# Gate, up and the gradient of h in one loop per 512 columns, half of the rows at a time, with relu(gate) and masked up kept in SBUF

## The chip, the cores and the metric

One core of a Trainium2 chip runs the whole program. The metric is the device time of one execution in microseconds (us). TensorE (PE) multiplies and transposes into PSUM, ScalarE (ACT) and VectorE (DVE) read PSUM and do the elementwise work, GpSimd (POOL) does little, and SyncE's queue (SP) issues nearly all DMAs, strictly in program order. For this kernel a difference under about 0.5% (11 us) can't be told from no change.

## The reference, cut to what matters

Forward and backward of a block with two branches on xn = layernorm(x), with S = 2048 rows, D = 1024 and F = 3584, all in bf16. The change is in branch B and its surroundings.

```python
gate = xn @ W_gate;  up = xn @ W_up              # [S, F]
h = relu(gate) * up
out = x + A(xn, k, v, ...) + h @ W_down
# backward, g = grad_out:
gh = g @ W_down.T                                # gradient of h, [S, F]
g_up = gh * relu(gate);  g_gate = gh * (gate > 0) * up
gW_down = h.T @ g;  gW_gate = xn.T @ g_gate;  gW_up = xn.T @ g_up
gx = ... + g_gate @ W_gate.T + g_up @ W_up.T     # through the layer norm
```

A is a shift convolution of k, a product with v, a long convolution over S (done as matrix Fourier transforms) and a product with xn, with its own gradients. It runs in 8 groups of 128 channels.

## The kernel before

Rows go in 16 tiles of 128 (`st`), D in 8 tiles of 128 (`kt`), F in 7 blocks of 512 columns (`fb`). A product of one row tile with one block is 8 matmuls of 512 columns into one PSUM tile (`gemm8`, L581). Four PSUM tiles (`b_ps`) go round for all of branch B.

Branch B goes through these phases, in this order: `layer_norm` (L520), `gate_up` (L589), `grad_hidden` (L611), `grad_down` (L667, gradient of W_down), `grad_in` (L685, gradients of W_gate and W_up), `out_phase` (L718, output 0) and `grad_x` (L753, gradient of x).

- `layer_norm` goes over chunks of 1, 1, 2, 4, 4 and 4 row tiles: two passes on ACT per tile (L537, L544), short steps on DVE, the scaling (L560), a store of xn to DRAM from POOL's queue (L562), 8 transposes on PE (L565) and a DVE copy to the tile `xnT` (L567). All 16 tiles `xnT` are made here, ahead of `gate_up` in PE's program. Then A's constant tables are made on DVE and ACT (`tables`, L103).
- `gate_up` does per block and row tile a gemm8 for gate and one for up. ACT takes relu (L603), DVE masks up (L604) and multiplies to h (L606). SP stores the pair relu/masked up to the DRAM buffer `ru_d` (L607) and h to `h_d` (L608).
- `grad_hidden` loads g transposed by DMA (`goT`, L617) and W_down's block transposed by DMA (`wdT`, L625), loads the pair back from `ru_d` (`rul`, L631), does one gemm8 (`ps_h`), copies it on ACT (`gh`, L635), multiplies the pair by it on DVE (L636) and stores it to `ug_d` (L639).
- `grad_down` loads g (`g_nat`, L656) and h (`hs`, slabs of 8 tiles, L647); `grad_in` loads xn (`xn_nat`) and the pair's gradients (`ugs`, L647) and writes its results from `wi` (L701).

Weights and slabs (wg, wu, wdT, hs, ugs) are tiles of 256 KB in one pool `w2` of 13 buffers; xnT, goT, g_nat and xn_nat share 16 buffers (`b_act`); ru, rul and the outputs share 5 (`b_e2`); ht and gh share 3 (`b_e1`).

Branch A is a generator of steps (`steps`, L375) that is interleaved into the phases of B: every gemm8 pays 1730 times the phase's pace into an account, and each step of A costs what it yields (about 121,000 for one group). A's matmuls stand in lines L64 and L266, its copies from PSUM in L68, its elementwise work in L72 and L277. A scheduler orders each engine's program from priorities; on the chip every engine then goes through its own list in order. When A is done, W_down is loaded for `out_phase`.

Of the kernel before, what the change touches and what calls it, by code (L numbers as in the profile page):

```python
# [39 lines left out]
NB1 = 32  # L40


class ABranch:
# [42 lines left out]
    def open(self):  # L86
# [16 lines left out]
    def tables(self):  # L103
# [117 lines left out]
    def loads_1(self, gi):  # L221
# [6 lines left out]
        for hf in range(2):  # L228
            rows = slice(8 * hf, 8 * hf + 8)
            xt = self.tap.tile([P, 8, P], BF16, name="xt", tag="tap")  # L230
            self.load(xt[:], xv[:, rows, :])
            self.tt(gt[:, rows, :], gt[:, rows, :], xt[:], ALU.mult)
        return dict(gi=gi, cg=cg, hn=hn, gt=gt)

    def loads_2(self, st):
# [9 lines left out]
        skb = self.sm.tile([P, 4, 1, P], BF16, name="skb")  # L245
# [129 lines left out]
    def steps(self):  # L375
# [4 lines left out]
        for gi in range(self.NG):  # L380
# [4 lines left out]
            yield from self.fwd1(hT, 2000, add_D=self.sDb[:, cg])  # L385
# [84 lines left out]
class LnMlp:  # L470
# [7 lines left out]
    def open_left(self):  # L478
# [3 lines left out]
        self.w2 = tc.alloc_tile_pool(name="b_w2", bufs=13, side="left")  # L482
        self.e2 = tc.alloc_tile_pool(name="b_e2", bufs=5, side="left")
# [26 lines left out]
    LN_CHUNKS = (1, 1, 2, 4, 4, 4)  # L510
# [9 lines left out]
    def layer_norm(self, x, xn_d, xpool, xtag, jpool, jtag, spool):  # L520
        nc, D, V = self.nc, self.D, self.nc.vector
        self.xnT = []
# [3 lines left out]
        for i, n in enumerate(self.LN_CHUNKS):  # L526
            if i == 1:
                self.ln_load(x, xpool, xtag, 5)
# [29 lines left out]
            for j in range(n):  # L558
# [27 lines left out]
    def gate_weights(self, Wg, Wu, fb):  # L586
        return self.col_block(Wg, fb, "wg"), self.col_block(Wu, fb, "wu")

    def gate_up(self, first, Wg, Wu, ru_d, h_d):  # L589
        nc = self.nc  # L590
        for fb in range(self.FB):
# [318 lines left out]
```

## Time and profile before

| what | value |
|---|---|
| median of 3 runs | 2192.49 us (2182.99 to 2195.03) |
| the profiled execution | 2189.52 us |
| its span, first to last instruction | 2187.8 us |
| PE busy | 1996.4 us, 91% of the span |
| DVE, ACT busy | 1013.9 us (46%), 697.2 us (32%) |
| DMA moved | 353.86 MB, 162 GB/s on average |

Busy PE counts pipelined matmuls by modelled ends, so a busy engine may still run at half clock; the granted clock stands in a row of its own, in tenths in the page and as a share in tables by stretch. The time outside the span is 1.7 us. "Idle before" in brackets is an engine's idle time ahead of an instruction, with what ended it. A DMA row in a timeline (SPq) shows the time that the queue took to issue, not the transfer. Some matmul records are missing, so a group of 896 shows as about 875.

### The profile page before, as it was taken

Reading aid. Unit: us, or ns where it says so; the run is one execution under the profiler, and the core shown is the slowest. Engines: PE = TensorE matmul, PEld = TensorE weight load, DVE = VectorE, ACT = ScalarE, POOL = GpSimd, SP = SyncE. Lnnn points to the kernel's source line nnn. Section 1 sums busy time; section 2 is a strip of 40 time slices with the busy share of each in tenths; the row PEclk is TensorE's granted clock in tenths of the full one; section 3 lists DMA queues with packets and bytes.
Section 4 is the critical chain, followed back from the end, with each engine's and each line's share of the span. In section 5 each row is a group of like instructions: output and inputs, shape, how many; then the busy total and the mean of one; then the engine's idle time right before and its main releaser. Section 6 shows DMA issues by size and latency. Waiting matters only on the chain.

```text
span 2187.8 us, 26505 instructions
## 1 busy us (share of the span) xinstructions
PE 1996.4 (91%) x10363; PEld 957.0 (44%) x10566; DVE 1013.9 (46%) x1479; ACT 697.2 (32%) x903; POOL 19.3 (1%) x46
## 2 busy tenths in 40 slices
PE   2899999899979869888989899899999999999998
PEld 2444454444434324444445445344444444444443
DVE  5848669559333338686857546100011213233223
ACT  6355364264323228375637374111100000000000
POOL 1000000000000000000000000000000000000000
PEclk9999999999999989999999999999999999999999
DMA  7443544656999983526363414953299854554442
GB/s 252 130 152 133 165 140 137 184 144 179 256 285 299 297 266 88 145 70 173 99 200 113 129 63 127 242 191 113 92 218 259 218 138 111 123 133 115 106 124 61
DMA packets 593726, 353.86 MB, mean 162 GB/s; under 512 B 413248, under 2 KB 534080, under 8 KB 593600
## 3 DMA queue, kind: packets, MB, share of 16 engines
q1 hardware_dynamic: 592320, 347.96, 56.8%
q0 software_dynamic: 1280, 4.20, 0.5%
q8 instruction: 82, 1.34, 0.3%
q14 instruction: 44, 0.36, 0.1%
HBM read 156.24 MB, written 124.80 MB: 128 GB/s over the span
## 4 chain that ended last, share of the span: by engine, by line
PE 66%; DVE 12%; DMA 12%; SPq 4%; ACT 3%; issue 3%; POOL 0%; DVEq 0%; ACTq 0%; POOLq 0%
PE ps_x L779 18%; PE ps_w L662 14%; PE ps_o L746 7%; PE ps_u L583 7%; PE ps_g L583 7%; PE ps_h L583 5%; PE ps L64 5%; DMA kp<-in_A_k_dram 2%; DVE flp L277 2%; DVE t L72 2%; PE ps_d L662 2%; DMA gks<-gks 2%; DVE tap L72 2%; DMA ug_d<-rul 2%; ACT G L68 1%
## 5 line engine op out<-in xcount | busy, mean ns | idle before, releaser
L662 PE MATMUL ps_w<-ugs,xn_nat 128*128 128x512 bf16 x1747 | 404.7, 383 | 15.5 <-DMA ugs<-ug_d 9.5
L662 PEld LDWEIGHTS <-xn_nat 128*128 128x128 bf16 x1792 | 174.8, 99 | 220.6 <-issue 21.0
L583 PEld LDWEIGHTS <-xnT 128*128 128x128 bf16 x1792 | 173.6, 99 | 218.0 <-issue 28.9
L662 PE MATMUL ps_d<-g_nat,hs 128*128 128x512 bf16 x867 | 214.6, 386 | 18.9 <-DMA hs<-h_d 17.0
L583 PE MATMUL ps_u<-wu,xnT 128*128 128x512 bf16 x872 | 215.4, 384 | 17.6 <-DMA wu<-in_B_W_up_dram 11.7
L583 PE MATMUL ps_h<-wdT,goT 128*128 128x512 bf16 x877 | 202.5, 389 | 25.4 <-DMA wdT<-in_B_W_down_dram 21.0
L583 PE MATMUL ps_g<-wg,xnT 128*128 128x512 bf16 x874 | 211.3, 382 | 2.7 <-DVE ru L604 0.9
L746 PE MATMUL ps_o<-wd,hT 128*128 128x512 bf16 x878 | 194.8, 381 | 5.4 <-DMA hT<-h_d 4.5
L779 PE MATMUL ps_x<-wgT,ggT 128*128 128x512 bf16 x878 | 197.5, 379 | 1.0
L779 PE MATMUL ps_x<-wuT,guT 128*128 128x512 bf16 x878 | 197.3, 379 | 0.9
L583 PEld LDWEIGHTS <-goT 128*128 128x128 bf16 x896 | 89.1, 100 | 135.6 <-issue 36.1
L748 DVE TENSOR_TENSOR o<-ps_o,ya 128x512 bf16<-128x512 f32 x32 | 21.3, 687 | 269.7 <-PE ps_o L746 269.7
L700 ACT CAST wi<-ps_w 128x512 bf16<-128x512 f32 x112 | 65.5, 585 | 247.4 <-PE ps_w L662 217.9
L636 DVE TENSOR_TENSOR rul<-rul,gh 128x1024 bf16<-128x1024 bf16 x112 | 77.0, 692 | 145.5 <-DMA rul<-ru_d 107.6
L746 PEld LDWEIGHTS <-hT 128*128 128x128 bf16 x896 | 87.9, 98 | 112.1 <-DMA hT<-h_d 5.9
L779 PEld LDWEIGHTS <-ggT 128*128 128x128 bf16 x896 | 87.7, 98 | 105.7
L779 PEld LDWEIGHTS <-guT 128*128 128x128 bf16 x896 | 87.7, 98 | 105.7
L662 PEld LDWEIGHTS <-hs 128*128 128x128 bf16 x896 | 85.5, 99 | 109.1 <-DMA hs<-h_d 20.0
L781 DVE CUSTOM_DVE_ANT_0 gx<-ps_x,gy 128x512 f32<-128x512 f32 x32 | 22.1, 691 | 227.3 <-PE ps_x L779 212.7
L603 ACT ACTIVATE ru<-ps_g 128x512 bf16<-128x512 f32 x112 | 66.8, 597 | 189.5 <-PE ps_g L583 145.9
L277 DVE STREAM_TRANSPOSE flp<-B 128x1024 f32<-128x1024 f32 x48 | 90.5, 1932 | 71.8 <-ACT B L68 71.8
L635 ACT CAST gh<-ps_h 128x512 bf16<-128x512 f32 x112 | 65.5, 585 | 163.4 <-PE ps_h L583 134.9
(159 smaller groups left out, 1842.2 us busy)
## 6 DMA issues: line engine op xcount, KB each, us to landing
ru_d<-ru SPq DMA_DIRECT2D x112, 256.0 KB, 2.0
rul<-ru_d SPq DMA_DIRECT2D x112, 256.0 KB, 3.7
ug_d<-rul SPq DMA_DIRECT2D x112, 256.0 KB, 4.1
ugs<-ug_d SPq DMA_DIRECT2D x112, 256.0 KB, 4.9
h_d<-ht SPq DMA_DIRECT2D x112, 128.0 KB, 2.7
hs<-h_d SPq DMA_DIRECT2D x56, 256.0 KB, 4.2
out_dram<-wi SPq DMA_DIRECT2D x56, 256.0 KB, 2.9
wg<-in_B_W_gate_dram SPq DMA_DIRECT2D x28, 256.0 KB, 5.1
```

Source lines behind the costliest of these rows:

```text
L64: self.nc.tensor.matmul(out, lhsT=lhsT, rhs=rhs, start=start, stop=stop)
L72: self.nc.vector.tensor_tensor(out=out, in0=in0, in1=in1, op=op)
L277: self.nc.vector.transpose(out=df[:, c0:c0 + 32, :], in_=sf[:, c0:c0 + 32, :])
L583: self.nc.tensor.matmul(ps[:], lhsT=xT[:, kt * P:(kt + 1) * P], rhs=w(kt), start=(kt == 0), stop=(kt == self.DT - 1))
L603: nc.scalar.activation(out=ru[:, 0, :], in_=ps_g[:], func=ACT.Relu)
L635: nc.scalar.copy(out=gh[:], in_=ps[:])
L636: nc.vector.tensor_tensor(out=ru[:], in0=ru[:], in1=gh[:].rearrange("p (o f) -> p o f", o=1).to_broadcast([P, 2, 512]), op=ALU.mult)
L662: self.nc.tensor.matmul(ps[:], lhsT=lhsT(st), rhs=rhs(st), start=(st == 0), stop=(st == self.ST - 1))
L700: nc.scalar.copy(out=wo[:, d, :], in_=ps[:])
L746: nc.tensor.matmul(ps[:], lhsT=hT[:, kt, :], rhs=self.wd[:, kt, oc], start=(kt == 0), stop=(kt == self.FT - 1))
L779: nc.tensor.matmul(ps[:], lhsT=T[:, kt, :], rhs=W[:, kt, oc], start=(i == 0), stop=(i == n - 1))
L781: V.tensor_tensor_reduce(out=gx[:, oc], in0=ps[:], in1=gy[:, oc], scale=1.0, scalar=0.0, op0=ALU.add, op1=ALU.add, accum_out=m[:, ob:ob + 1])
```

## The change

The two phases `gate_up` and `grad_hidden` become one, `hidden`. It goes over two halves of 8 row tiles, in each over the 7 blocks, and in each block over pairs of row tiles: gate for two tiles, up for two, gradient of h for two. The pair relu/masked up stays in its SBUF tile `ru` until the gradient has been multiplied in, so `ru_d` is gone with its 112 stores and 112 loads of 256 KB. Wg, Wu and the transposed Wd of each block are loaded once in each half (168 tiles of 256 KB where there were 84; 56 of them transposed by DMA where there were 28). The first half's 8 tiles `xnT` come from PE transposes as before, but traced between the first groups (`flip_xn`); the second half's 8 are loaded back from DRAM transposed by DMA, so 8 x 8 PE transposes and 8 DVE copies are gone. The normalisation's chunks are 1, 3, 4, 4, 4. The first block's wdT is loaded ahead of x's second chunk.

Buffers: `w2` has 16 buffers (13), `b_e2` 6 (5); A's pool `tap` is gone (xt takes one buffer of `tmp`), A's D vector is loaded per group for 32 partitions, and skb has one buffer. A's pace is 0.9 in `hidden`, where it was 1.0 and 0.72.

```diff
+        xt = self.tmp.tile([P, 16, P], BF16, name="xt", tag="tmp")
+        self.load(xt[:], xv)
+        self.tt(gt[:], gt[:], xt[:], ALU.mult)
+        sD = self.sm.tile([NB1, P], BF16, name="sD")
...
-        self.w2 = tc.alloc_tile_pool(name="b_w2", bufs=13, side="left")
-        self.e2 = tc.alloc_tile_pool(name="b_e2", bufs=5, side="left")
+        self.w2 = tc.alloc_tile_pool(name="b_w2", bufs=16, side="left")
+        self.e2 = tc.alloc_tile_pool(name="b_e2", bufs=6, side="left")
...
-    LN_CHUNKS = (1, 1, 2, 4, 4, 4)
+    LN_CHUNKS = (1, 3, 4, 4, 4)
...
-                pst = self.ps.tile([P, self.DT, P], BF16, name="pst_x", tag="bps")
-                for kt in range(self.DT):
-                    nc.tensor.transpose(pst[:, kt, :], xt[:, j, kt * P:(kt + 1) * P], self.ident[:])
-                xT = self.act_tile("xnT")
-                V.tensor_copy(out=xT[:], in_=pst[:].rearrange("p a b -> p (a b)"))
-                self.xnT.append(xT)
+                self.xn.append(xt[:, j, :])
...
+    def load_T(self, src, st, name):
+        t = self.act_tile(name)
+        self.nc.sync.dma_start_transpose(out=t[:].rearrange("p (a b) -> p a b", b=P),
+                                         in_=src[st * P:(st + 1) * P, :])
+        return t
...
+    def hidden(self, first, Wg, Wu, Wd, g, xn_d, h_d, ug_d):
+
+        nc, HS = self.nc, self.ST // 2
+        for half in range(2):
+            s0 = half * HS
             self.pri.now()
...
+            xT = [self.load_T(xn_d, s0 + i, "xnT") for i in range(HS)] if half else []
+            if not half:
+                xT += [self.flip_xn(0), self.flip_xn(1)]
+            gT = []
+            for fb in range(self.FB):
                 self.pri.now()
...
+                wg, wu, wd = first if fb + half == 0 else self.weights(Wg, Wu, Wd, fb)
+                for sp in range(0, HS, 2):
+                    self.pri.now()
+                    if len(gT) < HS:
+                        gT += [self.load_T(g, s0 + sp + s, "goT") for s in range(2)]
+                    ru = [self.e2_tile("ru") for _ in range(2)]
+                    for s in range(2):
+                        ps = self.ps_tile("ps_g")
+                        self.gemm8(ps, xT[sp + s], wg)
+                        nc.scalar.activation(out=ru[s][:, 0, :], in_=ps[:], func=ACT.Relu)
+                        yield 1730
+                        self.pri.now()
+                    for s in range(2):
+                        ps = self.ps_tile("ps_u")
+                        self.gemm8(ps, xT[sp + s], wu)
+                        ht = self.e1_tile("ht")
+                        nc.vector.scalar_tensor_tensor(out=ru[s][:, 1, :], in0=ru[s][:, 0, :], scalar=0.0, in1=ps[:],
+                                                       op0=ALU.is_gt, op1=ALU.mult)
+                        nc.vector.tensor_tensor(out=ht[:], in0=ru[s][:, 0, :], in1=ru[s][:, 1, :], op=ALU.mult)
+                        nc.sync.dma_start(out=h_d[(s0 + sp + s) * P:(s0 + sp + s + 1) * P, cols], in_=ht[:])
+                        yield 1730
+                        self.pri.now()
+                    if len(xT) < HS:
+                        xT += [self.flip_xn(len(xT) + s) for s in range(2)]
+                    for s in range(2):
+                        ps = self.ps_tile("ps_h")
+                        self.gemm8(ps, gT[sp + s], wd)
+                        gh = self.e1_tile("gh")
+                        nc.scalar.copy(out=gh[:], in_=ps[:])
+                        nc.vector.tensor_tensor(out=ru[s][:], in0=ru[s][:], in1=gh[:].rearrange(
+                            "p (o f) -> p o f", o=1).to_broadcast([P, 2, 512]), op=ALU.mult)
+                        nc.sync.dma_start(out=ug_d[(s0 + sp + s) * P:(s0 + sp + s + 1) * P, :, cols], in_=ru[s][:])
+                        yield 1730
+                        self.pri.now()
...
-        yield 1.0, b.gate_up(first, B_W_gate, B_W_up, ru_d, h_d)
-        yield 0.72, b.grad_hidden(B_W_down, g, ru_d, ug_d)
+        yield 0.9, b.hidden(first, B_W_gate, B_W_up, B_W_down, g, xn_d, h_d, ug_d)
```

DVE's program at the start, before: the last chunk's normalisation, A's tables (L118 to L211; `nb` is one of their columns), and then the first masking of up (L604).

```order
L556 RECIPROCAL rstd<-ln_s 128x4
L118 MEMSET negpi 128x1
L124 TENSOR_SCALAR b_i<-pidx 128x1
L560 TENSOR_SCALAR ln_x<-ln_x,rstd 128x1024 x4
...
L186 TENSOR_SCALAR qI<-qI 128x2048 x2
...
L211 COPY sk_t<-ps_sk 32x128
L604 SCALAR_TENSOR_TENSOR ru<-ru,ps_u 128x512 x2
L606 TENSOR_TENSOR ht<-ru 128x512 x2
```

DVE's program at the same place in the change (L551 is the old L556, L631 the old L604, L633 the old L606, L599 the copy of a transposed row tile, L644 the old L636).

```order
L644 TENSOR_TENSOR ru<-ru,gh 128x1024
L550 CAST ln_s<-ln_b 128x4
L551 RECIPROCAL rstd<-ln_s 128x4
L116 MEMSET negpi 128x1
...
L184 TENSOR_SCALAR qI<-qI 128x2048 x2
...
L209 COPY sk_t<-ps_sk 32x128
L644 TENSOR_TENSOR ru<-ru,gh 128x1024
L631 SCALAR_TENSOR_TENSOR ru<-ru,ps_u 128x512 x2
...
L599 COPY xnT<-pst_x 128x1024 x2
```

The tables still stand behind the last chunk's normalisation, but four maskings of up and three products with gh now stand ahead of them; the maskings of row tiles 4 and 5 (L631 x2) and the copies of tiles 6 and 7 (L599 x2) stand behind them.

SP's program at a change of block in `gate_up`, before: the pair and h of the last row tiles (L607, L608) between the next blocks' weights.

```order
L576 DMA wu<-in_B_W_up_dram 128x2x512
L607 DMA ru_d<-ru 128x1024
L608 DMA h_d<-ht 128x512
L576 DMA wu<-in_B_W_up_dram 128x2x512 x2
L576 DMA wg<-in_B_W_gate_dram 128x2x512
L607 DMA ru_d<-ru 128x1024
L608 DMA h_d<-ht 128x512
L576 DMA wg<-in_B_W_gate_dram 128x2x512 x3
```

SP's program at a change of block in `hidden` (L566 loads wg and wu, L581 wdT, L634 stores h, L646 the finished pair).

```order
L646 DMA ug_d<-ru 256x1x512 x2
L566 DMA wu<-in_B_W_up_dram 128x2x512 x4
L581 DMA_TRANSPOSE wdT<-in_B_W_down_dram 128x2x512 x2
L634 DMA h_d<-ht 128x512
L581 DMA_TRANSPOSE wdT<-in_B_W_down_dram 128x2x512
L634 DMA h_d<-ht 128x512
L581 DMA_TRANSPOSE wdT<-in_B_W_down_dram 128x2x512
```

The next block's wu and wdT stand where the old block's last up (its two h stores) is still to come, and the transposes are interleaved with those two stores.

SP's program at the end of `grad_hidden`, before: the g tiles and h slabs for `grad_down`.

```order
L656 DMA g_nat<-in_grad_out_dram 128x1024
L639 DMA ug_d<-rul 256x1x512
L656 DMA g_nat<-in_grad_out_dram 128x1024 x10
L647 DMA hs<-h_d 128x2x512 x13
```

SP's program at the end of `hidden` (L655 loads hs, L664 g_nat); the first four hs stand 28 rows ahead of the four shown.

```order
L664 DMA g_nat<-in_grad_out_dram 128x1024
L655 DMA hs<-h_d 128x2x512 x4
L664 DMA g_nat<-in_grad_out_dram 128x1024
L80 DMA skb<-sk_d 128x512
L655 DMA hs<-h_d 128x2x512
L634 DMA h_d<-ht 128x512
L664 DMA g_nat<-in_grad_out_dram 128x1024
```

The first slab of h stood behind all 16 g tiles; now it stands ahead of the last four.

## Rows read from the trace of the kernel before

**Rows 1.** The page: busy us (share of the span) xinstructions of each engine.

```profile
PE 1996.4 (91%) x10363; PEld 957.0 (44%) x10566; DVE 1013.9 (46%) x1479; ACT 697.2 (32%) x903; POOL 19.3 (1%) x46
```

**Rows 2.** PE's waits over the span: who waited for what, us, times, longest.

```profile
PE ps_h L583 <- DMA wdT<-in_B_W_down_dram: 21.0, 6, 4.6
PE ps L64 <- DVE flp L277: 20.2, 10, 5.2
PE ps_d L662 <- DMA hs<-h_d: 17.0, 1, 17.0
...
PE ps_u L583 <- DMA wu<-in_B_W_up_dram: 11.7, 7, 4.7
PE ps_w L662 <- DMA ugs<-ug_d: 9.5, 6, 3.3
```

**Rows 3.** Stretches: us, busy PE PEld DVE ACT POOL (xinstructions), granted clock, DMA share, GB/s.

```profile
85.00:545.00 460.00, 437.96 (x2431) 216.34 (x2478) 324.42 (x435) 214.28 (x260) 2.07 (x5) 0.98 0.51 154
...
597.00:779.00 182.00, 159.50 (x690) 70.43 (x703) 62.65 (x91) 52.98 (x92) 0.00 (x0) 0.94 0.99 295
779.00:796.00 17.00, 0.07 (x1) 0.08 (x2) 2.08 (x3) 0.51 (x1) 0.00 (x0) 0.56 1.02 339
796.00:802.00 6.00, 6.00 (x16) 1.98 (x17) 0.00 (x0) 0.00 (x0) 0.00 (x0) 0.54 1.09 348
...
1230.00:1400.00 170.00, 152.70 (x876) 75.12 (x892) 86.30 (x90) 74.64 (x90) 0.82 (x2) 0.95 0.46 130
```

**Rows 4.** DMA issues in 597 to 779 us: count, KB each, median us to landing.

```profile
rul<-ru_d SPq DMA_DIRECT2D x91, 256.0 KB, 3.6
```

**Rows 5.** Timeline of the start: start us, us, engine, instruction [idle before].

```profile
10.41 1.03 PE L565 MATMUL pst_x<-ident,ln_x 128*128 128x128 bf16 x8 [10.41 <-DVE ln_x L560]
...
12.23 1.06 ACT L537 ACTIVATE ln_j<-ln_x 128x1024 bf16<-128x1024 bf16 x1 [3.95 <-DMA ln_x<-in_A_q_dram]
...
46.54 1.67 DVE L560 TENSOR_SCALAR ln_x<-ln_x,rstd 128x1024 bf16<-128x1024 bf16 x4
...
57.63 1.68 DVE L560 TENSOR_SCALAR ln_x<-ln_x,rstd 128x1024 bf16<-128x1024 bf16 x4
...
61.22 1.89 PE L583 MATMUL ps_g<-wg,xnT 128*128 128x512 bf16 x7
62.95 1.89 PE L583 MATMUL ps_u<-wu,xnT 128*128 128x512 bf16 x8
...
76.98 1.26 DVE L604 SCALAR_TENSOR_TENSOR ru<-ru,ps_u 128x512 bf16<-128x512 bf16 x2
...
81.15 1.89 PE L583 MATMUL ps_g<-wg,xnT 128*128 128x512 bf16 x8
```

**Rows 6.** Timeline around 265 us: SP's queue, and PE's wait for wu.

```profile
265.20 1.46 SPq L576 DMA_DIRECT2D wu<-in_B_W_up_dram  x3
...
268.74 4.87 PE L583 MATMUL ps_u<-wu,xnT 128*128 128x512 bf16 x14 [4.75 <-DMA wu<-in_B_W_up_dram]
```

**Rows 7.** The whole span's DMA issues: count, (KB each,) median us to landing.

```profile
h_d<-ht SPq DMA_DIRECT2D x112, 128.0 KB, 2.7
...
wu<-in_B_W_up_dram SPq DMA_DIRECT2D x28, 256.0 KB, 5.6
...
wdT<-in_B_W_down_dram SPq DMA_TRANSPOSE x28, 4.9
```

**Rows 8.** Timeline of SP's queue: one DMA transpose issued.

```profile
566.18 1.38 SPq L625 DMA_TRANSPOSE wdT<-in_B_W_down_dram  x1
```

**Rows 9.** What SP's queue itself waited for, us, times, longest.

```profile
SPq L84 <- DVE gv L72: 20.0, 6, 8.2
SPq L84 <- DVE gk L72: 18.7, 3, 9.0
```

**Rows 10.** A stretch with two waits for wdT, ps_h's instructions alone: us, PE, ACT, clock, DMA.

```profile
617.00:629.00 12.00, 7.04 (x20) 1.25 (x3) 0.57 0.98 316
```

More of the change, by code (lines that the diff above doesn't have):

```diff
@@ L227, in loads_1 @@
         xv = self.tview(self.xn_d, cg)
[L228 to L233, printed above, removed]
+        xt = self.tmp.tile([P, 16, P], BF16, name="xt", tag="tmp")
+        self.load(xt[:], xv)
+        self.tt(gt[:], gt[:], xt[:], ALU.mult)
+        sD = self.sm.tile([NB1, P], BF16, name="sD")
+        self.load(sD[:], self.ssm_D[cg].partition_broadcast(NB1))
+        return dict(gi=gi, cg=cg, hn=hn, gt=gt, sD=sD)
     def loads_2(self, st):
@@ L244, in loads_2 @@
         self.load(vt[:], self.tview(self.v, cg))
-        skb = self.sm.tile([P, 4, 1, P], BF16, name="skb")
+        skb = self.sm.tile([P, 4, 1, P], BF16, name="skb", bufs=1)
         self.load(skb[:].rearrange("p i o c -> p (i o c)"),
@@ L384, in steps @@
             yield 2000
-            yield from self.fwd1(hT, 2000, add_D=self.sDb[:, cg])
+            yield from self.fwd1(hT, 2000, add_D=st["sD"])
             Hf = self.flipped
@@ L521, in layer_norm @@
         nc, D, V = self.nc, self.D, self.nc.vector
-        self.xnT = []
+        self.xn = []
         st0 = 0
@@ L584, in gemm8 @@
                                   stop=(kt == self.DT - 1))
[L586 to L591, printed above, removed]
-            self.pri.now()
-            cols = slice(fb * 512, fb * 512 + 512)
-            wg, wu = first if fb == 0 else self.gate_weights(Wg, Wu, fb)
-            for st in range(self.ST):
-                self.pri.now()
-                ps_g, ps_u = self.ps_tile("ps_g"), self.ps_tile("ps_u")
-                self.gemm8(ps_g, self.xnT[st], wg)
-                yield 1730
-                self.pri.now()
-                self.gemm8(ps_u, self.xnT[st], wu)
-                ru, ht = self.e2_tile("ru"), self.e1_tile("ht")
-                nc.scalar.activation(out=ru[:, 0, :], in_=ps_g[:], func=ACT.Relu)
-                nc.vector.scalar_tensor_tensor(out=ru[:, 1, :], in0=ru[:, 0, :], scalar=0.0, in1=ps_u[:],
-                                               op0=ALU.is_gt, op1=ALU.mult)
-                nc.vector.tensor_tensor(out=ht[:], in0=ru[:, 0, :], in1=ru[:, 1, :], op=ALU.mult)
-                nc.sync.dma_start(out=ru_d[fb, st], in_=ru[:].rearrange("p a f -> p (a f)"))
-                nc.sync.dma_start(out=h_d[st * P:(st + 1) * P, cols], in_=ht[:])
-                yield 1730
@@ new lines, in row_block_T, with weights @@
+    def row_block_T(self, W, fb, name):
+        out = []
+        for q in range(self.DT // 2):
+            t = self.w_tile(name)
+            self.nc.sync.dma_start_transpose(out=t[:], in_=W[fb * 512:(fb + 1) * 512, q * 256:(q + 1) * 256])
+            out.append(t)
+        return lambda kt: out[kt // 2][:, kt % 2, :]
+    def weights(self, Wg, Wu, Wd, fb):
+        return self.col_block(Wg, fb, "wg"), self.col_block(Wu, fb, "wu"), self.row_block_T(Wd, fb, "wdT")
+    def load_T(self, src, st, name):
[3 more added lines that the diff above has]
+        return t
@@ L853 @@
     b.ln_load(x, a.frm, "frm", 0)
-    first = b.gate_weights(B_W_gate, B_W_up, 0)
+    first = b.weights(B_W_gate, B_W_up, B_W_down, 0)
     b.layer_norm(x, xn_d, a.frm, "frm", a.tmp, "tmp", a.sm)
```

46 lines of the change are left out of this document (9 added, 37 removed).

## The prediction

> **What bounds the kernel now.** I read the page first: PE is busy 91% of the span, its nearest neighbour DVE 46%, so what counts is where PE stands still or runs slowly [rows 1]. The table by stretches shows that this isn't even: from 85 to 545 us PE is busy 438 of 460 us with the DMA engines half used, but from 597 to 779 it is busy only 159.5 of 182 us, at a granted clock of 0.94, with DMA at 0.99 and 295 GB/s. From 779 to 796 PE does nothing at all and DMA stands at 1.02 [rows 3]. The reader should see there that the second half of `grad_hidden` is bound by DMA: each gemm8 needs a 256 KB load of the pair and a 256 KB store of its gradient [rows 4], and a gemm8 takes 1.73 us (62.95 less 61.22 us, [rows 5]). 524 KB in 1.73 us would be 303 GB/s; 295 is what the engines moved. In the third view, PE's waits, I look for those that the change touches: `wdT` 21.0 us, `hs` 17.0, `wu` 11.7, `ugs` 9.5 [rows 2]. And at the start all products wait for the layer norm: the first `ps_g` stands at 61.22 us [rows 5].
>
> **What the change removes and adds, step by step.**
>
> *The pair's round trip.* 224 transfers of 256 KB go, 58.7 MB by their own size; 84 weight tiles of 256 KB come, 28 of them transposed, and 8 `xnT`: 24.1 MB. Per pair of row tiles (six gemm8, 10.4 us) SP stores two h and two pairs, 0.79 MB, 76 GB/s; per block and half (24 gemm8, 41.5 us) it loads 12 weight tiles, 3.15 MB, another 76 GB/s. With A that is about what the stretch of 85 to 545 us has now (154 GB/s, share 0.51, [rows 3]). So DMA is no longer a bound, and the waits that go with it can go.
>
> *wdT, 21.0 us in 6 waits.* The SP rows at a change of block show the next wdT issued while the old block's last up runs. From the end of that block's last gate product (time 0) the old wu tiles come free at 2 to 3.5 us, and four transposes at 1.38 us each [rows 8], two h stores between them, are issued by about 9 us; with 4.9 us to landing [rows 7] the last tile is there at 12 to 13. The first ps_h of the next block is ten gemm8 away minus two: u, u, h, h, g, g, u, u, 8 x 1.73 = 13.8 us, plus A's matmuls. That fits with about 1 to 2 us to spare.
>
> *wu, 11.7 us in 7 waits.* Now, wu's last tiles can only be issued when the last wg tile comes free, which is two gemm8 (3.5 us) ahead of the first use, and a wu takes 5.6 us to land [rows 7]: the row at 265.20 us shows three wu issued, and PE waiting 4.75 us for them until 268.74 [rows 6]. In the change u, u, h, h, g, g lie between: 10.4 us. This wait should go.
>
> *hs, 17.0 us.* The first slab stood behind 16 g tiles on SP, at a saturated DMA. Now four of its tiles are loaded a block earlier and four ahead of the last four g tiles. What is late next is the last g tile, whose buffer comes free with the last ps_h: I put 2.5 us for it, the nearest row being a 3.6 us landing [rows 4] less part of the 3.2 us that PE needs to reach the sixteenth matmul (15 x 0.216).
>
> These three are 49.7 us. I don't believe that 13 changes of block pass without any wait, since SP can stand up to 9 us for A's stores [rows 9]: I put 0.7 us each, 9 us. Bounds: nothing, and 13 x 3.5 = 45.5 us, the mean of today's wdT wait (21.0 / 6). 0.7 is nearer to the lower end because A's stores fall on a change of block only now and then. So 49.7 - 2.5 - 9 = 38.2 us.
>
> *ugs, 9.5 us in 6 waits.* Each slab of `grad_in` has 8 tiles; 13 buffers hold one slab and five tiles of the next, 16 hold both. The wait goes whole: 9.5 us.
>
> *The clock.* After such waits the granted clock falls to half: 0.57 over 617 to 629 us, with two waits in it [rows 10], 0.54 in the 6 us after the wait for hs [rows 3]. A stretch T at a granted clock c loses at most (1 - c)T of matmul time: 0.02 x 460 + 0.06 x 182 + 0.46 x 6 = 23 us from `gate_up` to `grad_down`'s start, and 0.05 x 170 = 8.5 us around the ugs waits [rows 3]. Part of it lies under the waits themselves or belongs to waits that stay (A's `flp`, 20.2 us, [rows 2]). I take about a third, 8 and 3 us, bounds 0 and 31. The Trainium skill, page "TensorE: Matmul & The Clock Gate", section "HAM oscillation — how this bites in real kernels", says that a product whose batches wait for DMA falls back to the low clock at each wait and starts the next batch cold. The trace agrees (0.57 and 0.54); without this term the gain would be 11 us less.
>
> *The start.* PE no longer waits for all 16 tiles. x's second chunk has three tiles and stands behind wdT. Today its like (one tile; ten transfers of 262 KB have landed with it) is there at 12.23 us [rows 5], which is 214 GB/s; six more are 1.57 MB, at 214 to 295 GB/s 7.3 to 5.3 us: 19 us. A chunk of four takes 11.1 us from scaling to scaling (46.54, 57.63, [rows 5]), so tiles 1 to 3 are ready at about 30 and, two transposed tiles later (1.03 us each, [rows 5]), the first ps_g starts at 32 us, 29 us sooner. But that lead isn't kept. The next chunks' scalings follow at 41, 53 and 66 us (11.1 each, and a little more for the relus, copies and products that now stand between), and behind the last one DVE makes A's tables: today that takes 76.98 - 57.63 = 19.4 us [rows 5] with four copies of xnT in it, so about 16, until 82 us. Behind them in DVE's rows stand the maskings of row tiles 4 and 5, whose PSUM tiles h4 and h5 need. So at 82 us PE has done 16 gemm8 (six gates, six ups, four h); today it is in its eleventh (eleven start from 61.22 to 81.15 us; the first two and the last are in [rows 5]). The lead is 5.5 x 1.73 = 9.5 us; the copies of tiles 6 and 7, also behind the tables, and the low clock after the stall take some 3 of it: 6 us. Bounds: 0, if the layer norm slips another 5 us behind the maskings on ACT and DVE; and 24 us, if PE ran through from 32 us (50 us less 8 of transposes are 24 gemm8, 13.7 ahead). I take 6, nearer to 0, since the order on DVE is fixed.
>
> *Costed at nothing.* The 8 transposes and copies saved are in the count above. A's pace: `hidden` pays 336 x 1730 x 0.9 = 523,000, the two phases paid 387,500 + 139,500 = 527,000, so A stands at the same step when `grad_down` begins; DVE has the same work. xt in `tmp`, skb with one buffer and sD wait for buffers that A frees well before; A's own chain hides that; without this cover each of the 8 groups would show a load's landing, 3.6 to 5.6 us [rows 4, 7], up to 45 us.
>
> **Sum.** 38.2 + 9.5 + 11 + 6 = 64.7 us off the profiled 2189.5: 2124.8. The median of the runs lies 3.0 above the profiled execution, so 2128.
>
> **Rivals.**
>
> *Weights late at each change of block.* For it: SP issues a transpose in 1.38 us, does everything in order, and now has 56 of them beside h stores that wait for DVE. At 3.5 us for 13 changes 36.5 us of the gain go, and most of the clock's 8: about 2170. Against it: the 8 gemm8 between issue and use. The Trainium skill's "Perfetto Trace Analysis", section "What “DMA-bound” means", names the issuing engine's sequencer as a bound of its own beside the DMA engines. No stretch of this trace shows it alone: where PE waited for wdT the DMA engines were at 0.99.
>
> *The start keeps its lead.* If PE isn't blocked by the tables, 18 us more: about 2110.
>
> *A takes the time back.* A's steps come 50 us sooner, and PE then waits for `flp` as it does after 796 us (20.2 us, [rows 2]). DVE is 0.71 busy in 85 to 545 [rows 3] and would be no fuller in `hidden`; if it still bound, half of the gain would go: about 2160.
>
> *Slower than before.* ht and gh share three buffers, and now alternate: the copy of the second ps_h of a pair needs the buffer of the first ht, so that h store must have landed. From the end of that up product: masking and product 1.1 us, issue 0.4, landing 2.7 [rows 7], 4.2 us; it is needed at 5.2 us (three gemm8), and PSUM forgives 4.6 more. If SP is late by over 5.6 us, PE stands. For a loss of 0.5% each of the 56 pairs would have to lose (64.7 + 11) / 56 = 1.4 us, 2204 or more. SP's long waits are nine in 38.7 us [rows 9], which can't reach that: hardly likely.
>
> **Chances.** The forecast, 2105 to 2150: 0.60. Weights late, 2150 to 2180: 0.16. The start's full lead, 2085 to 2105: 0.09. A takes it back, 2150 to 2180: 0.06. No change within 11 us: 0.05. Slower: 0.04. The range that leaves out 2 in 10 is 2100 to 2172. Faster by over 0.5% (about what a measurement of this kernel can tell from no change): 0.91; same 0.05; slower 0.04.
>
> **What would show it.** First ps_g near 32 us, then a stall of some 9 us near 73 to 82 while DVE makes tables; DMA share near 0.5 and clock near 1.0 all through `hidden`, with `ps_d` beginning near 796 - 38.2 - 8 - 6 = 744 us, where it began at 796 [rows 3]; PE's waits for wu and wdT under 10 us in total, for hs under 3, for ugs none; from `out_phase` on nothing changes. Waits for wdT of 3 us at each change of block, waits of SP ahead of h stores, or more `flp` waits would make the prediction wrong.

## The result, and the profile after

| | before | after |
|---|---|---|
| median | 2191.94 us (2182.99 to 2195.03, 4 runs) | 2112.02 us (2108.35 to 2113.93, 4 runs) |
| ratio to before, 95% interval | | 0.964 [0.9608, 0.9672] |
| profiled execution, its span | 2189.5, 2187.8 us | 2113.9, 2112.2 us |

The change is faster by 79.9 us. The forecast was 2128, its range 2100 to 2172; the largest miss among its steps is a term that it had at nothing.

First PE's waits in the kernel after, as in [rows 2]: who waited for what, us, times, longest.

```profile
PE ps L64 <- DVE hT L76: 34.7, 6, 9.6
PE ps_sk L207 <- DMA sk_b<-in_A_shift_k_dram: 17.0, 1, 17.0
PE pst_x L597 <- DVE ln_x L555: 12.4, 2, 10.6
PE ps_h L573 <- DVE ru L631: 11.7, 2, 10.4
PE ps_o L754 <- DMA hT<-h_d: 8.0, 2, 4.4
PE ps L64 <- ACT yt L68: 7.7, 2, 6.5
...
PE ps_d L670 <- DMA g_nat<-in_grad_out_dram: 4.0, 2, 2.2
...
PE ps_h L573 <- DMA wdT<-in_B_W_down_dram: 2.2, 2, 1.4
...
PE ps L64 <- DVE flp L274: 1.8, 2, 1.0
...
PE ps_u L573 <- DMA wu<-in_B_W_up_dram: 1.2, 1, 1.2
```

The waits that the change aimed at are gone: wdT 21.0 to 2.2, wu 11.7 to 1.2, hs 17.0 to nothing with 4.0 for g_nat in its place, ugs 9.5 to nothing ([rows 2] against these). So is one that it did not aim at, flp, 20.2 to 1.8. The largest group is now `hT`, DVE's copy of a flipped (transposed) h in A's branch. It was smaller in the kernel before:

```profile
PE ps L64 <- DVE hT L76: 15.3, 4, 7.5
```

So the waits for `flp` (DVE's transposes in A) fell by 18.4 us and those for `hT` grew by 19.4; over the whole span the two cancel.

Then the stretches, with the columns of [rows 3] (ps_d is the PSUM tile of `grad_down`'s products, ps_w that of `grad_in`'s, ps_o that of `out_phase`'s); the fused stage is 31.6 to 774.0, `grad_down` follows to 1056.4, `grad_in` to 1509.4, `out_phase` to 1716.7.

```profile
61.00:85.00 24.00, 13.56 (x67) 6.19 (x66) 22.06 (x68) 11.88 (x11) 2.41 (x5) 0.78 0.48 140
85.00:545.00 460.00, 438.02 (x2423) 213.46 (x2421) 314.17 (x415) 221.97 (x287) 2.07 (x5) 0.97 0.60 157
597.00:726.00 129.00, 123.90 (x709) 61.05 (x707) 95.05 (x126) 66.48 (x85) 0.82 (x2) 0.99 0.56 152
...
774.00:1056.40 282.40, 254.65 (x1529) 127.09 (x1528) 159.94 (x164) 140.67 (x167) 2.06 (x5) 0.96 0.44 126
1509.40:1716.70 207.30, 199.31 (x897) 88.90 (x896) 39.45 (x59) 0.59 (x1) 0.00 (x0) 0.97 0.91 206
```

Where the kernel before had DMA at 0.99 and 295 GB/s [rows 3], the fused stage has 0.56 to 0.60 and 152 to 157 GB/s.

**Stage by stage.** To see where the time came from I count, for each stage, the matmuls that stand in the program between its first product and the next stage's, at 0.216 us for 512 columns, 0.056 for 128 and 0.029 for 64 (the median distances from start to start in the trace). What the stage took beyond that is called lost: waits, and work at the low clock. In brackets is the part of the work that is A's, in us.

| stage | before: took (A), lost | after: took (A), lost |
|---|---|---|
| start, to the first ps_g | 61.2 (0.9), 53.1 | 31.6 (0), 30.6 |
| gate_up and grad_hidden, or hidden | 734.7 (72.6), 81.5 | 742.5 (96.0), 63.2 |
| grad_down | 326.5 (74.5), 58.4 | 282.4 (52.0), 36.8 |
| grad_in | 470.3 (49.6), 33.6 | 453.0 (49.6), 16.3 |
| out_phase | 200.0 (0), 6.5 | 207.3 (0), 13.8 |
| grad_x | 395.1 (0), 8.0 | 395.4 (0), 8.4 |

The row to look at is `grad_down`, whose own code the diff doesn't touch (its slabs do get more buffers): it is 44 us shorter, 22.5 because A's work stands earlier and 21.6 because less is lost. The trace shows the first half of that directly: these are PE's instructions of A's products alone (busy us, how many, clock, DMA share, GB/s), first `grad_hidden` and `grad_down` in the kernel before, then `hidden` and `grad_down` after.

```profile
545.20:795.90 250.70, 9.01 (x71) 0.93 0.98 288
795.90:1122.40 326.50, 94.30 (x852) 0.97 0.44 122
```

```profile
31.60:774.00 742.40, 123.12 (x1080) 0.97 0.61 163
774.00:1056.40 282.40, 65.84 (x601) 0.96 0.44 126
```

Before, A stood almost still in `grad_hidden` (71 products in 250 us) and caught up in `grad_down` (852), where PE then waited for A's `flp`. Of A's 2373 matmuls, with the transposes, 872 stand ahead of the first ps_d in the program before and 1144 in the change. That is PE's program as the scheduler wrote it, so A's place was lost before the chip ran anything. PE's waits inside `grad_down` add up to 35.7 us before (19.0 for `flp`, 1.7 for `hT`; without the 17.0 for hs, which end with its first product) and 22.6 after (1.0 and 16.4): 13 of the 21.6 us are fewer waits. The rest, with 632 of A's products there where 904 stood, is no wait that the view lists.

### The profile page after: what moved, and what is told of

The parts are those of the page before. It is cut to its first block, busy times and chain, and to the rows that moved or that the text cites. A ratio compares the mean times of both kernels' runs of the same rounds, so it can differ in the third digit from the quotient of the medians.

```text
span 2112.2 us, 26202 instructions
## 1 busy us (share of the span) xinstructions
PE 1983.0 (94%) x10502; PEld 947.0 (45%) x10502; DVE 1003.4 (48%) x1450; ACT 693.2 (33%) x902; POOL 20.1 (1%) x46
## 4 chain that ended last, share of the span: by engine, by line
PE 78%; DVE 7%; DMA 7%; ACT 4%; issue 2%; SPq 1%; DVEq 0%; POOL 0%; ACTq 0%
PE ps_x L787 18%; PE ps_w L670 16%; PE ps_o L754 9%; PE ps L64 7%; PE ps_u L573 7%; PE ps_g L573 7%; PE ps_h L573 7%; PE ps_d L670 6%; DMA kp<-in_A_k_dram 3%; DVE tap L72 1%; ACT H L68 1%; ACT G L68 1%; DMA gks<-gks 1%; DVE ksh L72 1%; DVE flp L274 1%
## 5 line engine op out<-in xcount | busy, mean ns | idle before, releaser
L573 PE MATMUL ps_h<-wdT,goT 128*128 128x512 bf16 x896 | 213.7, 385 | 13.9 <-DVE ru L631 11.7
L573 PE MATMUL ps_u<-wu,xnT 128*128 128x512 bf16 x896 | 209.8, 381 | 1.4 <-DMA wu<-in_B_W_up_dram 1.2
L754 PE MATMUL ps_o<-wd,hT 128*128 128x512 bf16 x896 | 199.5, 387 | 8.0 <-DMA hT<-h_d 8.0
L754 PEld LDWEIGHTS <-hT 128*128 128x128 bf16 x896 | 88.9, 99 | 118.4 <-DMA hT<-h_d 9.2
L68 ACT CAST B<-ps 128x1024 bf16<-128x1024 f32 x96 | 96.2, 1016 | 76.5 <-PE ps L64 76.3
L68 ACT CAST C<-ps 128x1024 bf16<-128x1024 f32 x96 | 96.7, 1019 | 51.0 <-PE ps L64 51.0
```

What stands on the lines that cost most here:

```text
L68: self.nc.scalar.copy(out=out, in_=in_)
L573: self.nc.tensor.matmul(ps[:], lhsT=xT[:, kt * P:(kt + 1) * P], rhs=w(kt), start=(kt == 0), stop=(kt == self.DT - 1))
L754: nc.tensor.matmul(ps[:], lhsT=hT[:, kt, :], rhs=self.wd[:, kt, oc], start=(kt == 0), stop=(kt == self.FT - 1))
```

## The experiments

My theory after the result: the pair's round trip on SyncE's queue had cost in two places, in `grad_hidden` itself, and in `grad_down`, which had to take what A could not do before. The rivals: the gain is the buffers that the change adds; or the bytes; or A's later place as such. Each ratio below is to runs of the kernel before taken alongside, whose medians were 2188.5 to 2191.2 us. Times that differ by 2 to 8 us among the kernels with the change (e3, e5, e6, e9, e12) lie under the 11 us that can't be told from no change, and their intervals overlap; for those the stages of the profiled executions are read beside them.

**The buffers alone, e1_buffers.** The kernel before with only the change's pools: `b_w2` 13 to 16, `b_e2` 5 to 6, and what pays for them in A's pools (`xt` in `tmp`, `skb` with one buffer, `sD` per group).

```diff
-self.w2 = tc.alloc_tile_pool(name="b_w2", bufs=13, side="left")
-self.e2 = tc.alloc_tile_pool(name="b_e2", bufs=5, side="left")
+self.w2 = tc.alloc_tile_pool(name="b_w2", bufs=16, side="left")
+self.e2 = tc.alloc_tile_pool(name="b_e2", bufs=6, side="left")
```

> The kernel before with the change's buffers alone (w2 16, e2 6, no tap, sD and skb as in the change). My theory: the waits for ugs (9.5 us) and wu (11.7 us) go with some 5 us of low clock, those for wdT (21.0) and hs (17.0) stay, since DMA is still saturated: about 2166 us, ratio 0.988. Rival: without the loop's new order the buffers are worth nothing in gate_up, only ugs goes: about 2180, ratio 0.995.

Measured: 2166.39 us (2163.49 to 2169.99), ratio 0.9889 [0.9867, 0.9911], 25 us faster than before. The number is the theory's; the waits are not, so that it came out so well is in part luck. Those for wu, wdT and ugs are all gone from the list, wdT's too, which was to stay. But `grad_hidden` still has DMA at 0.99, and other waits stand there and in `grad_down` (the first row is `grad_hidden`, with the columns of [rows 3]):

```profile
538.00:765.60 227.60, 203.99 (x950) 92.04 (x969) 77.79 (x110) 69.57 (x115) 0.41 (x1) 1.00 0.99 281
```

```profile
PE ps_h L580 <- ACT gh L632: 21.3, 24, 2.0
PE ps L64 <- DVE flp L274: 19.5, 10, 4.3
...
PE ps_d L659 <- DMA g_nat<-in_grad_out_dram: 10.2, 2, 5.8
PE ps_d L659 <- DMA hs<-h_d: 6.4, 1, 6.4
```

The 21.3 us for gh stand in the place of wdT's 21.0: ACT waits 122.6 us for DVE's products of the pair, and DVE 126.0 us for the pair's loads. The 17.0 for hs became 16.6 for g_nat and hs, now behind the first ps_d, so `grad_hidden` loses 26.6 us for 49.8 and `grad_down` 79.0 for 58.4. Together that is 3 us less; what the buffers gained is 7 us in `gate_up` and 13 in `grad_in` (20.5 for 33.6). So the buffers do not bring A back, they only rename the waits of the saturated DMA, and the rest of the gain isn't theirs.

**The same size taken out of the change, e12_old_buffers.**

```diff
-self.w2 = tc.alloc_tile_pool(name="b_w2", bufs=16, side="left")
-self.e2 = tc.alloc_tile_pool(name="b_e2", bufs=6, side="left")
+self.w2 = tc.alloc_tile_pool(name="b_w2", bufs=13, side="left")
+self.e2 = tc.alloc_tile_pool(name="b_e2", bufs=5, side="left")
```

> The change with the buffers of before: 13 for weights instead of 16, and 5 for pairs of columns instead of 6. Each block of columns has 12 tiles of weights, so that one buffer is free for the next block in place of four. My theory: what hides the weights' loads in the fused stage is mostly these buffers, as it was in the kernel before (25 us with the same edit made there): W_up's and W_down's blocks come late again at 13 changes of block, 1 to 2.5 us each, 2112 + 13 x 1.7 = 2134 us, between 2124 and 2146, and the new waits are for wu or wdT in the fused stage. Rival: the fused stage asks for so little a us that the loads are in time with one buffer too: 2108 to 2118 us.

Measured: 2120.24 us (2115.94 to 2124.81), ratio 0.9685 [0.9658, 0.9712]: 8 us more than the change, near the rival. In the fused stage the loss grows by 2.8 us only (66.0 for 63.2); 10.6 come in `grad_in` (26.9 for 16.3), which has a wait of 6.2 for ugs again. These rows are of this kernel:

```profile
PE ps_h L573 <- DMA wdT<-in_B_W_down_dram: 8.7, 10, 1.8
...
PE ps_w L670 <- DMA ugs<-ug_d: 6.2, 2, 6.1
```

The fused stage asks for so little a us that one free buffer nearly does; it is `grad_in` that gains by the sixteen (the sixth buffer of pairs went with them and was not taken out by itself).

**No reload, e2_no_reload.** The kernel before, whose `grad_hidden` does not load the pair.

```diff
-nc.sync.dma_start(out=ru[:].rearrange("p a f -> p (a f)"), in_=ru_d[fb, st])
...
-nc.vector.tensor_tensor(out=ru[:], in0=ru[:],
-                        in1=gh[:].rearrange("p (o f) -> p o f", o=1).to_broadcast([P, 2, 512]),
-                        op=ALU.mult)
+ghb = gh[:].rearrange("p (o f) -> p o f", o=1).to_broadcast([P, 2, 512])
+nc.vector.tensor_tensor(out=ru[:], in0=ghb, in1=ghb, op=ALU.mult)
```

> The kernel before, but grad_hidden doesn't load the pair back: it multiplies gh by itself instead, so the gradients that follow are of other numbers; the stores to ru_d stay. My theory: the saturated DMA cost two things, PE's waits (wdT 21.0 and most of hs 17.0, with some 8 us of low clock) and the place of A, whose late stores and steps found no room in grad_hidden: 1152 of A's matmuls stand ahead of ps_d in the program where it was 872, so grad_down waits some 20 us less. About 2133 us, ratio 0.973. Rival: only the waits count, what A does earlier costs as much there as it saves later: about 2152, ratio 0.982.

Measured: 2120.74 us (2117.14 to 2123.37), ratio 0.9679 [0.9661, 0.9697]: 70 us faster, more than either theory gave. A is back (1152 of its matmuls ahead of ps_d), and its products by stage, `grad_hidden` and `grad_down`, are:

```profile
541.70:781.50 239.80, 39.72 (x332) 0.98 0.71 197
781.50:1055.20 273.70, 64.15 (x588) 0.97 0.44 129
```

`grad_hidden` loses 14.6 us for 49.8 with 24 us more of A's work in it, and `grad_down` 29.8 for 58.4. Leaving out this load in the old loops is worth nearly as much as the whole change. The other half of the round trip, the 112 stores to `ru_d`, was not taken out by itself.

**The load on another queue, e11_pair_by_pool.** No reload leaves out the bytes and the place on the queue at once. This run separates them: the bytes stay, and GpSimd issues the load.

```diff
-nc.sync.dma_start(out=ru[:].rearrange("p a f -> p (a f)"), in_=ru_d[fb, st])
+nc.gpsimd.dma_start(out=ru[:].rearrange("p a f -> p (a f)"), in_=ru_d[fb, st])
```

> The kernel before with one edit: the load of the pair in the gradient of h is issued by GpSimd and not by SyncE. Bytes, waits for buffers and pace are the same. The program then has 1152 of A's matmuls ahead of grad_down, as the kernel without the reload had, where the kernel before has 872. My theory: what held A up in that pass was one queue, SyncE's, on which A's loads and stores stood behind a load and a store of each step; with the load on another queue A keeps its place and grad_down its cover: 2125 to 2150 us. Rival: the bytes and the late loads of W_down's blocks are the cost, whoever issues: within 12 us of before, 2178 to 2200 us.

Measured: 2166.0 us (2154.86 to 2176.13, 6 runs), ratio 0.99 [0.9868, 0.9932]: 22 us faster, outside both. A's products in `grad_hidden` and `grad_down`, and PE's wait in the former:

```profile
546.60:827.30 280.70, 39.70 (x332) 0.94 0.93 264
827.30:1104.20 276.90, 63.23 (x588) 0.95 0.46 136
```

```profile
PE ps_h L583 <- ACT gh L635: 15.6, 7, 6.1
```

The result divides into my theory and the rival. `grad_down` is as without the reload: 277.0 us, 33.1 lost for 58.4. A's 1152 matmuls ahead of ps_d are in the program again, so A's place is a matter of the queue that the load stands on, and the loss in `grad_down` follows it; how the scheduler comes to that order isn't shown. `grad_hidden` is not: with A's products in it and the bytes still there (DMA 0.93, 264 GB/s) it loses 55.5 us, for 49.8. PE waits for gh, ACT 118.4 us for DVE's products of the pair, and GpSimd 119.9 us for a store of the pair to land before it can load into its buffer. So there the transfers cost, through the five buffers of pairs; bytes and buffers are not separated there.

**The bytes put back, e7_dummy_load.** Do bytes cost in the fused stage too? The pool `e3` has one buffer.

```diff
+rul = self.e3.tile([P, 1024], BF16, name="rul", tag="e3")
+nc.sync.dma_start(out=rul[:], in_=g[(s0 + sp + s) * P:(s0 + sp + s + 1) * P, :])
 ps = self.ps_tile("ps_h")
```

> The change with one more load of 256 KB in each step of the hidden stage (a block of rows of the gradient of the output, which nothing reads; its buffer comes out of the weights' pool, 15 instead of 16): the bytes of the pair's reload are back, 29 MB, but spread over the whole fused stage and not packed into 250 us. My theory: what cost the kernel before its time was the packing of load and store into the short pass of the gradient of h, which starved A of transfers there, not the bytes as such: spread thin they cost little, 2112 to 2122 us, with A's matmuls ahead of grad_down unchanged. Rival: the bytes are the cost wherever they stand: the time goes back by what leaving out the reload gave the kernel before (70 us), 2160 to 2185 us. Between the two, 2130 to 2150, would say that both count.

Measured: 2170.0 us (2161.52 to 2171.97), ratio 0.99 [0.987, 0.993]. That is the rival's number. But the rows tell of something else than bytes: what SyncE's queue waited for, what PE waited for, and the group of the copies of gh with what ended ACT's idle time (this line is of the page's groups).

```profile
SPq L642 <- DMA rul<-in_grad_out_dram: 158.0, 80, 5.1
```

```profile
PE ps_u L574 <- ACT gh L646: 16.9, 9, 5.0
```

```profile
L646 ACT CAST gh<-ps_h 128x512 bf16<-128x512 f32 x112 | 65.6, 586 | 308.7 <-DMA h_d<-ht 154.5
```

The dead load's buffer is free only when the load before it has landed, and SyncE stands there. The stores of ht stand behind it, ht and gh share three buffers, and so ACT waits for h stores before it can copy gh (154.5 us, 56.7 in the change), and PE for ACT (16.9 us, 0.2 in the change). `hidden` loses 113 us for 63.2, with 13 us more of waits for weights among them. This is the chain that the prediction had as the way to a slower kernel.

**The same bytes without a wait, e10_dead_copy.**

```diff
+nc.sync.dma_start(out=ru_d[fb * self.ST + s0 + sp + s], in_=g[(s0 + sp + s) * P:(s0 + sp + s + 1) * P, :])
 ps = self.ps_tile("ps_h")
```

> The change with one dead copy of 256 KB from DRAM to DRAM in each step of the hidden stage, 112 in all, issued on SyncE like the dead load before, but with no tile: SyncE has to wait for nothing to issue it. In the run with the dead load SyncE waited 158.0 us in all (80 times) for the one buffer of that load, and the time was 2170.0. My theory: those waits on SyncE, with the stores of ht and ru behind them, made the 58 us and not the 29 MB: 2112 to 2125 us. Rival: the bytes make it (here read and written): 2150 to 2185 us.

Measured: 2124.59 us (2119.87 to 2125.81), ratio 0.9708 [0.9671, 0.9745], at the upper end of the theory's range. 112 issues and 29 MB, read and written, on the same queue cost 13 us (SyncE waits 5.7 us for them); the loads, 80 of them with a wait in front, cost 58. The same chain is at work here too, weaker: ACT waits 104.5 us for h stores in `hidden`, and

```profile
PE ps_u L573 <- ACT gh L644: 9.1, 3, 3.8
```

The two runs differ in one thing more, since the copies write to DRAM and the loads to SBUF; that was not tried by itself. The one buffer of weights that the dead load also took is hardly the difference: three of them and a pair's were worth 8 us. The Trainium skill, "Perfetto Trace Analysis", section "What “DMA-bound” means", counts the issuing sequencer as a bound when its track is full of DMA slices. No run here shows that: SyncE's 158 us were waits for a semaphore with nothing being issued.

**The start: e3_flips_first and e5_tables_late.** First all eight row tiles of xn flipped ahead of the first product, then, by itself, A's tables traced late (the edit stands at the top of `tables()`).

```diff
-xT += [self.flip_xn(0), self.flip_xn(1)]
+xT += [self.flip_xn(i) for i in range(HS)]
```

> The changed kernel with all eight transposed row tiles made ahead of the first product, as before. My theory: the first ps_g starts near 45 us instead of 31.6, but the tables on DVE hold PE until about 83 us either way, so nothing or up to 5 us is lost: 2112 to 2117, ratio 0.964 to 0.966. Rival: the early start is worth what it gains at first: 13 us more, 2125, ratio 0.970.

Measured: 2116.84 us (2115.15 to 2117.46), ratio 0.9661 [0.9646, 0.9676]. The first ps_g starts at 45.0, 13.4 us later than in the change, and the time is 4.8 us longer, within the theory's range. But the profiled execution doesn't bear out its reason. At 95 us PE has done 17 gemm8 where the change has 22, and ps_d begins at 783.6 us, 9.6 later than in the change; 5.3 of that come back only in `out_phase` (202.0 for 207.3), which the edit doesn't touch. So most of what the early start gives is kept until ps_d, nearer to the rival.

```diff
 nc, con, big, pri = self.nc, self.con, self.big, self.pri
-pri.now()
+pri.late()
```

> The change with the tables of A's branch built at the late priority instead of the early one, so that the masked-up and product steps of the first blocks stand ahead of them on VectorE. My theory: the one wait of the first ps_h for VectorE (10.4 us at 83 us of the span in the changed kernel) goes, and with it the low clock behind it (some 10 us at half speed, 5 us), and A starts no later than its first loads allow: 2112 - 15 + 2 = about 2099 us, between 2096 and 2104, a ratio to the changed kernel of 0.994. Rival: the tables are only built later and A's first products wait for them on TensorE, in program order ahead of other work: the 10 us come back as one wait for A's tables, 2108 to 2116 us.

Measured: 2105.82 us (2101.09 to 2107.02), ratio 0.961 [0.9586, 0.9634]. That lies between the two ranges. The wait of 10.4 us for `ru` is gone from the list; ps_d begins 4.7 us sooner, and the gain of 6.2 us is half of what I expected. Against it stands sk_b, now waited for inside the stage:

```profile
PE ps_sk L207 <- DMA sk_b<-in_A_shift_k_dram: 5.8, 1, 5.8
```

**A's pace, e4_pace_low.** My next theory was that A's lag as such crowds `grad_down`.

```diff
-yield 0.9, b.hidden(first, B_W_gate, B_W_up, B_W_down, g, xn_d, h_d, ug_d)
+yield 0.7, b.hidden(first, B_W_gate, B_W_up, B_W_down, g, xn_d, h_d, ug_d)
```

> The changed kernel with A's pace 0.7 in hidden instead of 0.9: 856 of A's matmuls stand ahead of ps_d, about as many as in the kernel before (872), where the change has 1144. My theory: grad_down is crowded by A again and loses some 20 us to its waits (flp, hT), hidden gains less than that: about 2130 us, ratio 0.972. Rival: A's place is a wash: 2112 within 5 us, ratio 0.964.

Measured: 2100.18 us (2097.47 to 2103.49), ratio 0.9587 [0.9569, 0.9605]: faster by 12 us, where both expected slower or the same. With 856 of A's matmuls ahead of ps_d the lag is that of the kernel before, and yet `grad_down` is short. A's products in `hidden`, `grad_down` and `grad_in`:

```profile
31.70:729.60 697.90, 92.19 (x803) 0.98 0.63 167
729.60:1004.60 275.00, 62.17 (x588) 0.96 0.44 128
1004.60:1501.90 497.30, 93.63 (x837) 0.97 0.48 143
```

So a lag that is planned goes on to `grad_in`; it was the backlog against the plan, 852 products at once, that crowded `grad_down`. A's products cost `hidden` about what they weigh again: 22.9 us fewer of them there lose 21.8 us less (41.4 for 63.2). But they cost that in `grad_in` too, which has 24.6 us more of them and loses 19.5 more (35.8 for 16.3). So moving them gains 2 us there; 5 more are `grad_down`'s (31.5 for 36.8) and 3 `out_phase`'s, and why these are shorter isn't shown.

**A's copy of hT: e6_copy_early, e8_pace_tables_copy, e9_swap.**

```diff
-self.vcopy(hT[:, 0:16, :], pst[:])
+self.pri.now()
+self.nc.vector.tensor_copy(out=hT[:, 0:16, :], in_=pst[:])
```

> The change with the copy of A's flipped h (the DVE copy of hT out of PSUM) at the early priority instead of the late one. In the changed kernel this copy ended 34.7 us of TensorE's waits, the largest group, 6 over 2 us. My theory: the copy stands too far back on VectorE behind other work, put ahead it saves most of that: waits for hT under 10 us, time 2112 - 25 = about 2087, between 2080 and 2097 us. Rival: VectorE is the limit there and the wait only changes its name (ru, flp and yt grow by what hT loses): 2107 to 2117 us.

Measured: 2109.76 us (2105.17 to 2112.22), ratio 0.9629 [0.96, 0.9659]: nothing. My theory falls, and the rival's reason too, since the wait keeps its name (38.1 us). VectorE's timeline in this run, ahead of the longest of these waits:

```profile
931.65 1.23 DVE L72 TENSOR_TENSOR ksh<-kp,skb 128x2048 bf16<-128x2048 bf16 x1 [11.48 <-DMA kp<-in_A_k_dram]
932.79 2.35 DVE L72 TENSOR_TENSOR tap<-kp,skb 128x2048 bf16<-128x2048 bf16 x2
935.06 2.48 DVE L72 TENSOR_TENSOR ksh<-ksh,tap 128x2048 bf16<-128x2048 bf16 x2
937.46 1.22 DVE L265 COPY hT<-pst 128x2048 bf16<-128x2048 bf16 x1
```

VectorE itself stands idle 11.5 us for k, with the taps (the products and sums of A's shift convolution) ahead of the copy: "PE waits for DVE" hides a DMA.

> Three edits of the change at once: A's pace 0.7 in the fused stage (alone 2100.2 us), the tables at the late priority, and the copy of hT at the early one. If the three gains add up: 2100 - 13 for the tables - 10 for the copy (there is less of that wait left at the lower pace) = about 2077, between 2068 and 2088 us. Rival: each only moves the same waits about, and the sum is no better than the lower pace alone: 2095 to 2105 us.

The edits are those above. Measured: 2094.76 us (2092.41 to 2098.28), ratio 0.9565 [0.9542, 0.9589], outside the theory's range and at the edge of the rival's: the gains of the pace (12 us) and the tables (6) add up, and the copy adds nothing.

In e9 the copy is back, and in each of A's groups work stands between the flips of h and their use (the pace of 0.7 and the late tables stay):

```diff
 hT = self.h_tile(st)
 yield 2000
-yield from self.fwd1(hT, 2000, add_D=st["sD"])
-Hf = self.flipped
+yield from self.fwd1(gt, 2000)
+Gf = self.flipped
...
-yield from self.fwd1(gt, 2000)
-Gf = self.flipped
-H = self.form("H")
-yield from self.fwd2(Hf, H, 1700)
+yield from self.fwd1(hT, 2000, add_D=st["sD"])
+Hf = self.flipped
+G = self.form("G")
+yield from self.fwd2(Gf, G, 1700)
```

> The change with A's pace 0.7 in the fused stage, the tables late, and in each of A's groups the first transform of the gradient ahead of that of h, so that eight slots of TensorE stand between the flips of h and their first use. (The copy of hT is at its old priority.) With the early priority for the copy nothing had moved: in the changed kernel VectorE ran the taps of the next group (4 products, 3 sums of 1.2 us) just ahead of the copy, in one place after 11.5 us of waiting for k. My theory: the wait for hT is one for a place on VectorE behind the taps, and work put between hides it: the 31 us of waits for hT in the run with three edits (2094.8 us) fall under 8, and 15 to 25 us of the time with them: 2075, between 2068 and 2082 us. Rival: VectorE's lag is the limit and not the place of one copy: the wait comes back as one for flp, G or H, and the time stays at 2090 to 2100 us.

Measured: 2087.24 us (2083.05 to 2088.33), ratio 0.954 [0.951, 0.9571], the fastest here, between the theory's range and the rival's. That is 7.5 us less than the run before, half of the smallest gain that I expected: the wait is down from 31.3 us to

```profile
PE ps L64 <- DVE hT L76: 17.8, 3, 7.3
```

Three of six are left, not under the 8 us foretold; that k is what is late in these too is not shown.

## Why the prediction was right, and where it was wrong

- **The pair's round trip, right in kind.** No wait of PE's that a transfer ended is left in `hidden` but 2.2 us for wdT and 1.2 for wu. The residue was put at 9 us for 13 changes of block; it is 3.4. For the last g tile 2.5 were foreseen, 4.0 measured. The rival of late weights falls with that, and e12 shows that even 13 buffers would only lose 3 us there. That the second half of `grad_hidden` was bound by DMA, e1 bears out: with more buffers the waits change their names, and DMA stays at 0.99.
- **The start, right.** First ps_g at 31.56 us (32 foretold). The stall behind the tables is this row, 9 us near 73 to 82 foretold:

```profile
83.16 5.45 PE L573 MATMUL ps_h<-wdT,goT 128*128 128x512 bf16 x16 [10.44 <-DVE ru L631]
```

  At 95 us PE has done 22 gemm8, 18 before: 6.9 us of lead, 6 foretold. The rival that keeps the whole lead falls; e3, which gives up the early start and has 17 by then, shows that the 6.9 us are the early start's.
- **The failed step: "so A stands at the same step when `grad_down` begins", costed at nothing.** The sum of paces is the same, 523,000 and 527,000, but the pace only says when A's steps are written. In the kernel before, with the pair's load on SyncE's queue, 872 of A's matmuls were ahead of ps_d, not 1144; without that load (e2), or with it on another queue (e11), 1152 are. The 20.2 us for flp, which the prediction took as staying, were the sign of it: 19.0 of them stood in `grad_down`. `grad_down` lost 21.6 us less, and in e2 and e11, too, it loses 25 to 29 less.
- **`ps_d` at 744 us, wrong for the same reason.** It began at 774.0, with 22.5 us more of A's work ahead of it (96.0 against 72.6 and 0.9 in the table); without that work it would be 751.5. So start and `hidden` gave 44 us of the 52 foretold. The 8 us that are missing are less than the 21.8 us of loss that as much of A's work costs there in e4; PE waits in `hidden` for `hT` 10.6 us and `yt` 6.5, and which of these the 8 are isn't shown. The signs were near: DMA at 0.61 (0.5 foretold) and the clock at 0.97 over `hidden`.
- **ugs and the clock around it**: 12.5 foretold, `grad_in` lost 17.3 us less. That the ugs wait is a matter of buffers e1 and e12 show from both sides.
- **The clock**: 11 us foretold. Stretches at a granted clock under 0.9 add up to 113 us before and 93 after; at the lower of the two levels, half speed, 20 us less of them are up to 10 us of matmul time, part of it under waits. `hidden` has 41 us of them where `gate_up` and `grad_hidden` had 52, `grad_in` 10 for 24, `out_phase` 14 for 3. In `hidden` they fall to 10 us with the lower pace and the late tables (e8, e9), whose waits are fewer.
- **"From `out_phase` on nothing changes"**: `out_phase` took 7.3 us more in the profiled execution, with 8.0 us of waits for h_d (4.5 before). In the other kernels with a fused stage it took 201.6 to 204.4, so 2 to 4 of the 7 repeat. The cause stays open.
- **Slower than before**, the rival: its chain through ht, gh and SyncE exists. Waits of SP ahead of h stores, named as a sign against the prediction, are there in the change too, in `hidden`

```profile
SPq L634 <- DVE ht L633: 170.6, 68, 8.0
```

  and ACT waits 56.7 us for h stores, but PE only 0.2 us for gh: the slack that the rival was weighed against was enough. In e10 PE's wait is 9.1 us, and it took the 158 us of waits for a buffer of e7 to make it 16.9.

In the sum: 52 + 0 + 12.5 foretold, 44.4 + 21.6 + 17.3 - 7.7 measured by stages, 64.7 against 75.6 us of the span. The misses are 8 us too much, 22 and 5 too little and 8 too much. That they cancel to 11 is luck, and the rest of the 16 us is that the median of the runs lies 1.9 us below the profiled execution, where I had put it 3 above.

## What to carry to other kernels

When a stage takes out traffic, look at who shares its queue and where that work went instead: the largest unforeseen gain here lay one stage later, in work that had fallen behind its plan, and a wait there that looks like another branch's affair (flp) is the sign of it. Here an extra transfer cost little where its issue waited for nothing, and much where an in-order queue stood still for its buffer (13 against 58 us for as many transfers of the same size). When buffers make a wait vanish, look for its new name before counting it as gained (e1). Before a copy is moved up because TensorE waits for it, read what its own engine waited for just ahead.

## What the runs showed of the hardware that I had not expected

GpSimd took 0.548 us for each of the pair's 112 loads, 61.4 us in all, and the loads took 4.3 us from issue to landing where they had taken 3.7 from SyncE's queue; and yet the kernel was 22 us faster (e11). And 112 copies of 256 KB from DRAM to DRAM, in a stage with DMA at 0.61 (0.71 with them), cost the kernel only 13 us (e10).
